# W2 loaded by column halves around batch 1's loads, half output tiles, W1's means spread between blocks, and batch 1's q transposed by DMA

## Chip, cores, metric

One core of one Trainium2 chip. The metric is the device time of one execution in microseconds (us), the median of several runs. Profiles show a span about 1 to 2 us shorter than the timed run.

## The reference

Eight batches. Attention with a memory of 32 slots per head, then a layer norm without shift and a two-layer block with residual:

```python
a = softmax(phi)                          # [8, 8, 576, 32]
k_m = einsum('bhsm,bhsd->bhmd', a, k)     # pooled keys; v_m alike
attn = softmax(q @ k_m.T / sqrt(64))
x = (attn @ v_m) -> [8, 576, 512]
xn = (x - mean) / sqrt(var + 1e-6) * g_ln
out = x + relu(xn @ w_ch1) @ w_ch2        # w_ch1 [512, 2048], w_ch2 [2048, 512]
```

## The kernel before

The kernel never forms xn: it multiplies the pooled values with W1 for each batch (w1b), corrected by the means of W1 (m_sb), and scales by the inverse deviation at the end. TensorE (PE) does for each batch: pooling (kv_ps), transposes of the pooled k and v (kvT), the w1b blocks, scores (sc_ps), denominators (den_ps), the first layer (mm1, h_ps) and, for pairs of batches, the second (mm2, ch_ps). ScalarE (ACT) and VectorE (DVE) do the copies, exponentials, additions and products between them; e are the exponentials of phi, es and hl their sums, Eh the scaled attention weights that enter the first layer. The order on each engine is the order of the program. GpSimd (POOL) issues the loads that cast fp32 to bf16, and phi of batch 1, in this order:

```python
# q, k, v of batch 0 (cut), then:
for fs in W1C:                                    # W1 in five column blocks
    nc.gpsimd.dma_start(out=w1r[:, :, fs], in_=w1_v[:, :, fs])
for n in range(4):
    w2_load(n)                                    # W2 in four row blocks of 512 KB (bf16)
phi1 = load_phi(1, nc.gpsimd)
kv1 = load_kv(1)
q1 = load_q(1)                                    # two halves
# ... and load(2): phi, k, v, q of batch 2, further down in the program
```

q has to be transposed for the scores. Batches 2 to 7 do it by DMA from SP's queue, batches 0 and 1 on PE:

```python
def a_qT(b, i):
    q_bf = loaded[b][2]
    if i == 0:
        qTs[b] = att.tile([P, 4, NP, P], BF16, name="qT")
    if b > 1:
        nc.sync.dma_start_transpose(out=qTs[b].rearrange("p j n x -> p (j n) x"),
                                    in_=q_bf.rearrange("p j n x -> p (j n x)"))
        return
    ...                                           # ten transposes on PE, then copies by ACT or DVE
```

The part of the program that the change rewrites, after batch 0's first layer:

```python
mm2(0, 0, 0, 4)          # second layer, tile 0, blocks 0 to 3 of 16; 512 columns
mm2(0, 1, 0, 4)
...
a_exp(1)                 # exponentials of phi, batch 1
mm2(0, 0, 4, 16)
mm2(0, 1, 4, 16)
mm2(0, 2, 0, 8)
a_kv(1)                  # pooling
mm2(0, 2, 8, 12)
a_tr(1)
a_qT(1, 0)
a_w1b(1, 0)
mm2(0, 2, 12, 16, finish=False)
a_qT(1, 1)
a_w1b(1, 1)
a_sc(1)                  # scores: the first use of qT
mm2_out(0, 2)
mm2(0, 3, 0, 4)
a_w1b(1, 2)
a_den(1)                 # denominators, and the products Eh
load(2)
a_exp(2)
...                      # tile 3, then mm1(1): batch 1's first layer
```

The softmax here doesn't subtract the row's maximum and nothing guards it: scores larger than these inputs give would overflow.

Of the kernel before, what the change touches and what calls it, by code (L numbers as in the profile page):

```python
# [9 lines left out]
FP32 = mybir.dt.float32  # L10
# [6 lines left out]
def kernel(  # L17
# [11 lines left out]
    nc = tc.nc  # L29
# [71 lines left out]
    w2b = consts.tile([P, JC, C], BF16, name="w2b")  # L101
    w2_v = moe_w_ch2.rearrange("(j p) c -> p j c", p=P)

    def w2_load(n):
        nc.gpsimd.dma_start(out=w2b[:, 4 * n:4 * (n + 1), :], in_=w2_v[:, 4 * n:4 * (n + 1), :])


    phi0 = load_phi(0)
# [27 lines left out]
    for fs in W1C:  # L136
        nc.gpsimd.dma_start(out=w1r[:, :, fs], in_=w1_v[:, :, fs])
    for n in range(4):
        w2_load(n)
    phi1 = load_phi(1, nc.gpsimd)  # L140
    kv1 = load_kv(1)
    q1 = load_q(1)
    loaded[1] = (phi1, kv1, q1)

    g_bf = consts.tile([P, 4], BF16, name="g_bf")
    gneg = consts.tile([P, 4, P], BF16, name="gneg")
# [37 lines left out]
    def a_exp(b):  # L184
        phi_st, kv, _ = loaded[b]
        e = att.tile([P, NS, 4, M], BF16, name="e_sb")
        nc.scalar.activation(out=e.rearrange("p c j m -> p j c m"),  # L187
                             in_=phi_st.rearrange("p j (c m) -> p j c m", m=M), func=AF.Exp)
        st8[b] = {"e": e, "kv": kv}
        if b >= 2:  # L190
            es = att.tile([P, P], FP32, name="es")
            ev = e.rearrange("p c j m -> p c (j m)")
            a4 = att.tile([P, 4, P], FP32, name="es4", bufs=1)
            nc.gpsimd.tensor_tensor(out=a4, in0=ev[:, 0:4], in1=ev[:, 4:8], op=ALU.add)  # L194
            a2 = att.tile([P, 2, P], FP32, name="es2", bufs=1)
            nc.gpsimd.tensor_tensor(out=a2, in0=a4[:, 0:2], in1=a4[:, 2:4], op=ALU.add)
            nc.gpsimd.tensor_tensor(out=es, in0=a2[:, 0], in1=a2[:, 1], op=ALU.add)
            nc.gpsimd.tensor_tensor(out=es, in0=es, in1=ev[:, 8], op=ALU.add)
            hl = att.tile([P, 2, P], BF16, name="hl")
            nc.gpsimd.tensor_copy(out=hl[:, 0], in_=es)  # L200
            nc.gpsimd.tensor_tensor(out=hl[:, 1], in0=es, in1=hl[:, 0], op=ALU.subtract)
            st8[b]["es"] = hl
# [40 lines left out]
        a_pool(b, ps)  # L243

    def a_sum(b, ps):
        if b < 2:
            kv_sum(b, ps)
        else:

            for i in range(2):  # L250
                nc.tensor.matmul(ps[:, 0, P:P + 2], st8[b]["es"][:, i, :], ones8,
                                 start=(i == 0), stop=(i == 1))
# [39 lines left out]
    def a_qT(b, i):  # L292
        q_bf = loaded[b][2]
        if i == 0:
            qTs[b] = att.tile([P, 4, NP, P], BF16, name="qT")
        if b > 1:

            nc.sync.dma_start_transpose(out=qTs[b].rearrange("p j n x -> p (j n) x"),
                                        in_=q_bf.rearrange("p j n x -> p (j n x)"))
            return  # L300
        split = b == 1 and i == 1
        if split:

            qs = [f([P, 1024], BF16, "qT_ps") for f in (big, one)]
        else:
            q_ps = big([P, 2, 1024], BF16, "qT_ps")
            qs = [q_ps[:, u, :] for u in range(2)]
        for u in range(2):
            for n in range(NP):
                nc.tensor.transpose(qs[u][:, P * n:P * (n + 1)], q_bf[:, 2 * i + u, n, :], ident)  # L310
        dst = qTs[b][:, 2 * i:2 * i + 2].rearrange("p a n x -> p a (n x)")
        if split:
            nc.scalar.activation(out=dst[:, 0], in_=qs[0][:, 0:NP * P], func=AF.Copy)
            nc.vector.tensor_copy(out=dst[:, 1], in_=qs[1][:, 0:NP * P])
        elif i == 0 or b == 1:
            nc.scalar.activation(out=dst, in_=q_ps[:, :, 0:NP * P], func=AF.Copy)
        else:
            nc.vector.tensor_copy(out=dst, in_=q_ps[:, :, 0:NP * P])
# [18 lines left out]
    def a_den(b, finish=True):  # L337
# [29 lines left out]
        if finish:  # L367
            a_den2(b)

    def a_den2(b):  # L370
        s = st8[b]
        Eh, rd = s["Eh"], s["rd"]
        for g in range(2):
            nc.scalar.activation(out=rd[:, g], in_=rd[:, g], func=AF.Exp, scale=-1.0)  # L374
            nc.vector.scalar_tensor_tensor(  # L375
                out=Eh[:, g, :], in0=s["E"][:, g, 0:S],
                scalar=s["rs"][:, g:g + 1], in1=rd[:, g].rearrange("p a x -> p (a x)"),
                op0=ALU.mult, op1=ALU.mult)

    def a_w1b(b, n, part=None):  # L380
        s = st8[b]
        if n == 0 and part in (None, 0):
            s["w1b"] = att.tile([P, 2, F], BF16, name="w1b", bufs=1)
        ps = big([P, 2, 512], FP32, "w1b_ps")
        fs = slice(512 * n, 512 * (n + 1)) if part is None else W1C[part]
        N = fs.stop - fs.start
        for j in range(4):
            for g in range(2):
                r = 64 * g
                nc.tensor.matmul(  # L390
                    ps[32 * j:32 * (j + 1), g, 0:N], s["kvT"][r:r + 64, 2, 32 * j:32 * (j + 1)],
                    w1r[r:r + 64, j, fs], start=True, stop=True, tile_position=(r, 32 * j))
        for g in range(2):
            nc.vector.scalar_tensor_tensor(  # L394
                out=s["w1b"][:, g, fs], in0=m_sb[:, fs], scalar=s["rsum"][:, g:g + 1],
                in1=ps[:, g, 0:N], op0=ALU.mult, op1=ALU.add)


    pair = {}
# [1 line left out]
    def mm1(b, j0, j1):  # L401
        s = st8[b]
        if b % 2 == 0 and j0 == 0:
            pair[b // 2] = moe.tile([P, JC, 2 * S], BF16, name="rT", bufs=1)
        rT = pair[b // 2]
        off = S * (b % 2)
        for j in range(j0, j1):
            h_ps = big([P, 2, 512], FP32, "h_ps")
            for g in range(2):
                for half in range(2):  # L410
                    nc.tensor.matmul(  # L411
                        h_ps[:, half, 0:HS], s["w1b"][:, g, P * j:P * (j + 1)],
                        s["Eh"][:, g, HS * half:HS * (half + 1)],
                        start=(g == 0), stop=(g == 1))
            dst = rT[:, j, off:off + S].rearrange("p (a x) -> p a x", a=2)
            if j % 3 != 1 if b == 0 else j % 3 or j == 0:
                nc.scalar.activation(out=dst, in_=h_ps[:, :, 0:HS], func=AF.Relu)  # L417
            else:
                nc.vector.tensor_scalar(out=dst, in0=h_ps[:, :, 0:HS], scalar1=0.0, scalar2=None,  # L419
                                        op0=ALU.max)  # L420
# [72 lines left out]
    def mm2(pr, t, j0, j1, ps=None, finish=True):  # L493
# [7 lines left out]
        if j1 == JC and finish:  # L501
            mm2_out(pr, t)

    def mm2_last(pr, t):

        x, rstd = xs[(pr, t)]
        for cs in (slice(0, 384), slice(384, 512)):
            ps = big([P, 2, 512], FP32, "last_ps")
            N = cs.stop - cs.start
            for j in range(JC):  # L510
                nc.tensor.matmul(ps[:, 0, 0:N], pair[pr][:, j, P * t:P * (t + 1)], w2b[:, j, cs],  # L511
                                 start=(j == 0), stop=(j == JC - 1))
            nc.vector.scalar_tensor_tensor(out=x[:, cs], in0=ps[:, 0, 0:N], scalar=rstd,
                                           in1=x[:, cs], op0=ALU.mult, op1=ALU.add)
            for u, queue in ((0, nc.sync), (1, nc.scalar)):
                lo = P * t + TS * u
                dst = out[2 * pr + lo // S].rearrange("(p c) x -> c p x", c=NS)
                queue.dma_start(out=dst[CO[lo % S // TS]][:, cs], in_=x[TS * u:TS * (u + 1), cs])

    def mm2_out(pr, t):  # L520
        ch_ps = chs[(pr, t)]
        x, rstd = xs[(pr, t)]
        nc.vector.scalar_tensor_tensor(out=x, in0=ch_ps, scalar=rstd, in1=x,  # L523
                                       op0=ALU.mult, op1=ALU.add)
        for u in range(2):
            lo = P * t + TS * u
            dst = out[2 * pr + lo // S].rearrange("(p c) x -> c p x", c=NS)
# [34 lines left out]
    a_w1b(0, 0, 1)  # L562
    warm(1, 256)
    mm1(0, 0, 2)
    w1_mean(2)
    m_copy(2)
    a_w1b(0, 1)
    mm1(0, 2, 5)
    w1_mean(3)
    m_copy(3)  # L570
    a_w1b(0, 2)
    mm1(0, 5, 8)
    w1_mean(4)
    m_copy(4)
    a_w1b(0, 3)
    mm1(0, 8, 11)
    a_vb(0)
    mm1(0, 11, 16)

    x_tiles(0, [0, 1])  # L580
    x_tiles(0, [2, 3])
    mm2(0, 0, 0, 4)
    mm2(0, 1, 0, 4)
    x_rstd(0, [0, 1])
    x_rstd(0, [2, 3])
    a_exp(1)
    mm2(0, 0, 4, 16)
    mm2(0, 1, 4, 16)
    mm2(0, 2, 0, 8)
    a_kv(1)  # L590
    mm2(0, 2, 8, 12)
    a_tr(1)
    a_qT(1, 0)
    a_w1b(1, 0)
    mm2(0, 2, 12, 16, finish=False)
    a_qT(1, 1)
    a_w1b(1, 1)
    a_sc(1)
    mm2_out(0, 2)
    mm2(0, 3, 0, 4)  # L600
    a_w1b(1, 2)
    a_den(1)
    load(2)
    a_exp(2)
    mm2(0, 3, 4, 12)
    a_w1b(1, 3)
    mm2(0, 3, 12, 16, finish=False)
    a_vb(1)
    mm2_out(0, 3)

    a_qT(2, 0)
    late = []
# [126 lines left out]
```

## Time and profile before

| | |
|---|---|
| time, median of 3 (range) | 250.08 us (249.71 to 250.16) |
| span of the profiled execution | 249.0 us |
| PE busy, share of the span | 95% |
| PE in the chain that ended last | 89% |
| first score matmul of batch 1 | 48.81 us |
| end of batch 1's first layer (next ch_ps) | 63.1 us |

The chain of waits is followed back from the last instruction: at each step to what released it. Time on another engine or on a DMA in that chain is time PE stood for. A transfer has landed when the trace shows it complete.

### The profile page before, as it was taken

The page shows a single profiled execution, that of the slowest core. Times are in us where ns is not written, and L with a number is a line of the kernel's source. Part 1 is how long each engine was busy: PE and PEld are TensorE (multiplying, and loading weights), DVE is VectorE, ACT ScalarE, POOL GpSimd, SP SyncE. Part 2 cuts the span into 40 slices and gives each one's busy share as a digit, 9 for nine tenths or more (in the row PEclk, how much of TensorE's full clock was granted, in tenths as well). Part 3 has the DMA queues.
Part 4 walks back from the last instruction along what each step waited for, and adds up shares of the span by engine and source line. Part 5 has one row for each costly group of instructions (what it writes and reads, how often), then busy time and mean ns, then how long its engine had stood idle before and what let it go on. Part 6 is the DMA issues. An engine that isn't in the chain of part 4 may idle for free.

```text
span 249.0 us, 5843 instructions
## 1 busy us (share of the span) xinstructions
PE 237.1 (95%) x2452; PEld 133.0 (53%) x2483; DVE 156.5 (63%) x304; ACT 129.8 (52%) x219; POOL 60.8 (24%) x100
## 2 busy tenths in 40 slices
PE   7879999999999999999999999999999999999994
PEld 2445454547644675457544674466544764476442
DVE  3228655586487655687569637685679538783641
ACT  3154583487554474838472556645580755465210
POOL 8643241014324502081206302180205001000000
PEclk9988999999999999999999999999999999999999
DMA  6999999996799799919975996629973301203133
GB/s 143 192 202 206 207 255 208 292 220 108 166 158 250 101 217 238 192 25 181 265 125 128 137 237 153 133 27 219 224 147 88 77 10 43 45 15 72 42 84 84
DMA packets 42450, 36.82 MB, mean 148 GB/s; under 512 B 17460, under 2 KB 37688, under 8 KB 42424
## 3 DMA queue, kind: packets, MB, share of 16 engines
q0 software_dynamic: 17776, 19.53, 46.9%
q1 hardware_dynamic: 24488, 16.79, 28.8%
q8 instruction: 19, 0.31, 0.5%
q10 hardware_dynamic: 160, 0.13, 0.2%
q14 instruction: 7, 0.06, 0.1%
HBM read 41.42 MB, written 9.44 MB: 204 GB/s over the span
## 4 chain that ended last, share of the span: by engine, by line
PE 89%; DMA 4%; ACT 2%; issue 2%; POOL 1%; DVE 1%; POOLq 0%
PE ch_ps L499 48%; PE h_ps L411 25%; DMA kv_bf<-in_v_dram 4%; PE w1b_ps L390 3%; PE kv_ps L210 2%; PE o_ps L442 2%; PE last_ps L511 1%; PE sc_ps L328 1%; PE m_ps L165 1%; PE den_ps L359 1%; ACT rT L417 1%; PE w_ps L179 1%; POOL q_bf L92 1%; ACT E_sb L333 1%; DVE w1b L394 1%
## 5 line engine op out<-in xcount | busy, mean ns | idle before, releaser
L499 PE MATMUL ch_ps<-w2b,rT 128*128 128x512 bf16 x531 | 123.0, 379 | 1.9 <-issue 1.1
L499 PEld LDWEIGHTS <-rT 128*128 128x128 bf16 x560 | 52.4, 98 | 63.2 <-issue 6.5
L411 PE MATMUL h_ps<-Eh,w1b 128*128 128x288 bf16 x512 | 66.3, 285 | 1.0 <-ACT rT L417 1.0
L417 ACT ACTIVATE rT<-h_ps 128x576 bf16<-128x576 f32 x88 | 52.2, 648 | 26.3 <-PE h_ps L411 26.3
L411 PEld LDWEIGHTS <-w1b 128*128 128x128 bf16 x512 | 49.5, 97 | 17.7 <-issue 2.0
L394 DVE SCALAR_TENSOR_TENSOR w1b<-m_sb,rsum,w1b_ps 128x512 bf16<-128x512 f32 (+1 forms) x66 | 44.2, 727 | 7.1 <-PE w1b_ps L390 4.7
L419 DVE TENSOR_SCALAR rT<-h_ps 128x576 bf16<-128x576 f32 x40 | 30.3, 758 | 25.3 <-PE h_ps L411 24.7
L523 DVE SCALAR_TENSOR_TENSOR x_sb<-ch_ps,rstd,x_sb 128x512 f32<-128x512 f32 x35 | 26.1, 746 | 9.7 <-PE ch_ps L499 5.4
L479 DVE BATCH_NORM_STATS2 bst<-x_sb 128x6 f32<-128x512 f32 x36 | 24.4, 678 | 8.8 <-ACT x_sb L450 8.8
L450 ACT ACTIVATE x_sb<-o_ps 128x1024 f32<-128x1024 f32 x16 | 16.0, 1027 | 18.2 <-PE o_ps L442 18.2
L287 POOL TENSOR_TENSOR vb<-v,vmask 128x256 bf16<-128x256 bf16 x12 | 7.8, 665 | 60.1 <-DVE rs L237 60.1
L194 POOL TENSOR_TENSOR es<-e_sb 128x512 f32<-128x512 bf16 x6 | 6.9, 1154 | 63.2 <-ACT e_sb L187 63.2
L485 ACT ACTIVATE rstd<-mv,eps_sb 128x2 f32<-128x2 f32 (+1 forms) x20 | 5.9, 297 | 30.5 <-DVE mv L480 30.3
L333 ACT ACTIVATE E_sb<-sc_ps,rs 128x640 bf16<-128x640 f32 x16 | 11.8, 790 | 11.8 <-PE sc_ps L328 11.8
L375 DVE SCALAR_TENSOR_TENSOR Eh<-E_sb,rs,rden 128x576 bf16<-128x576 bf16 x16 | 12.4, 815 | 8.8 <-ACT rden L374 8.8
L179 PE MATMUL w_ps<-fill 128*128 128x512 f32 (+1 forms) x16 | 10.5, 776 | 1.6 <-DVE fill L119 1.6
L390 PE MATMUL w1b_ps<-w1r,kvT 64*32 64x512 bf16 (+1 forms) x264 | 11.0, 378 | 0.2
L227 DVE CAST k<-kv_ps 128x256 bf16<-128x256 f32 x7 | 3.0, 425 | 12.5 <-PE kv_ps L210 12.5
L187 ACT ACTIVATE e_sb<-phi_st 128x1152 bf16<-128x1152 f32 x8 | 9.2, 1151 | 2.6 <-DMA phi_st<-in_phi_dram 2.6
L374 ACT ACTIVATE rden<-rden 128x576 f32<-128x576 f32 x16 | 10.0, 673 | 0.1
L92 POOL DMA_DIRECT2D q_bf<-in_q_dram x10 | 7.6, 756 | 4.6 <-DMA w2b<-in_moe_w_ch_dram 1.8
L210 PE MATMUL kv_ps<-kv_bf,e_sb 64*32 64x128 bf16 (+1 forms) x648 | 7.4, 215 | 0.6 <-DMA kv_bf<-in_v_dram 0.3
(79 smaller groups left out, 155.2 us busy)
## 6 DMA issues: line engine op xcount, KB each, us to landing
out_dram<-x_sb SPq DMA_DIRECT2D x70, 128.0 KB, 3.2
kv_bf<-in_k_dram POOLq DMA_DIRECT2D x7, 576.0 KB, 6.0
kv_bf<-in_v_dram POOLq DMA_DIRECT2D x7, 576.0 KB, 9.8
phi_st<-in_phi_dram SPq DMA_DIRECT2D x6, 576.0 KB, 5.0
q_bf<-in_q_dram POOLq DMA_DIRECT2D x6, 576.0 KB, 14.0
w2b<-in_moe_w_ch_dram POOLq DMA_DIRECT2D x4, 512.0 KB, 17.1
w1r<-in_moe_w_ch_dram POOLq DMA_DIRECT2D x3, 512.0 KB, 13.2
q_bf<-in_q_dram POOLq DMA_DIRECT2D x4, 288.0 KB, 12.8
```

The source lines that it names most:

```text
L179: nc.tensor.matmul(w_ps[:, 0:N], fill[:, 0:P], fill[:, 0:N], start=True, stop=True)
L333: nc.scalar.activation(out=E_[:, g].rearrange("p (a x) -> p a x", a=2), in_=sc[:, :, 0:HP], func=AF.Exp, scale=s["rs"][:, g:g + 1])
L375: nc.vector.scalar_tensor_tensor(out=Eh[:, g, :], in0=s["E"][:, g, 0:S], scalar=s["rs"][:, g:g + 1], in1=rd[:, g].rearrange("p a x -> p (a ...
L390: nc.tensor.matmul(ps[32 * j:32 * (j + 1), g, 0:N], s["kvT"][r:r + 64, 2, 32 * j:32 * (j + 1)], w1r[r:r + 64, j, fs], start=True, stop=Tru ...
L394: nc.vector.scalar_tensor_tensor(out=s["w1b"][:, g, fs], in0=m_sb[:, fs], scalar=s["rsum"][:, g:g + 1], in1=ps[:, g, 0:N], op0=ALU.mult, o ...
L411: nc.tensor.matmul(h_ps[:, half, 0:HS], s["w1b"][:, g, P * j:P * (j + 1)], s["Eh"][:, g, HS * half:HS * (half + 1)], start=(g == 0), stop= ...
L417: nc.scalar.activation(out=dst, in_=h_ps[:, :, 0:HS], func=AF.Relu)
L419: nc.vector.tensor_scalar(out=dst, in0=h_ps[:, :, 0:HS], scalar1=0.0, scalar2=None, op0=ALU.max)
L450: nc.scalar.activation(out=x[:, 0:n].rearrange("p i (u y) -> p i u y", u=2), in_=o_ps.rearrange("p u (i y) -> p i u y", i=2)[:, 0:n], func ...
L479: nc.vector.bn_stats(out=stt, in_=x)
L499: nc.tensor.matmul(ch_ps, rT[:, j, P * t:P * (t + 1)], w2b[:, j, :], start=(j == 0), stop=(j == JC - 1))
L523: nc.vector.scalar_tensor_tensor(out=x, in0=ch_ps, scalar=rstd, in1=x, op0=ALU.mult, op1=ALU.add)
```

## The change

The intent: with only half of W2 ahead of them, batch 1's loads land earlier, so there is time to transpose its q by DMA, which takes 20 transposes and their copies off PE, ACT and DVE. Since only W2's first 256 columns are there, the output tiles 0 to 3 are computed by halves, first halves first. W1's means are placed in smaller pieces between blocks of the first layer. Batch 1's exponential sums move to GpSimd, as in later batches.

```diff
-    def w2_load(n):
-        nc.gpsimd.dma_start(out=w2b[:, 4 * n:4 * (n + 1), :], in_=w2_v[:, 4 * n:4 * (n + 1), :])
+    C2 = (slice(0, C // 2), slice(C // 2, C))
+    def w2_load(h, n):
+        nc.gpsimd.dma_start(out=w2b[:, 4 * n:4 * (n + 1), C2[h]],
+                            in_=w2_v[:, 4 * n:4 * (n + 1), C2[h]])
@@
     for n in range(4):
-        w2_load(n)
+        w2_load(0, n)
     phi1 = load_phi(1, nc.gpsimd)
     kv1 = load_kv(1)
     q1 = load_q(1)
     loaded[1] = (phi1, kv1, q1)
+    for n in range(4):
+        w2_load(1, n)
@@ a_exp; a_sum likewise
-        if b >= 2:          # sums of the exponentials on GpSimd (es, hl)
+        if b >= 1:
@@ a_qT
-        if b > 1:           # q transposed by DMA
+        if b > 0:
@@ new: half output tiles, two halves to a bank
+    def mm2h(t, h, j0, j1):
+        if j0 == 0 and (h == 1 or t % 2 == 0):
+            halfs[h] = one([P, 2, C // 2], FP32, "ch_ps")
+        if j0 == 0:
+            chs[(t, h)] = halfs[h][:, 0 if h else t % 2, :]
+        for j in range(j0, j1):
+            nc.tensor.matmul(chs[(t, h)], pair[0][:, j, P * t:P * (t + 1)],
+                             w2b[:, j, C2[h]], start=(j == 0), stop=(j == JC - 1))
@@ W1's means, e.g.
     mm1(0, 0, 2)
-    w1_mean(2)
+    w1_mean(2, 0, 2)
+    mm1(0, 2, 3)
+    w1_mean(2, 2, 4)
     m_copy(2)
@@ the order after batch 0's first layer (new)
+    a_exp(1)
+    mm2h(0, 0, 0, 16)
+    ...                     # first halves of tiles 0 to 3
+    a_kv(1)
+    a_qT(1, 0)
+    mm2h(0, 1, 0, 4)
+    a_tr(1)
+    mm2h(1, 1, 0, 4)
+    a_w1b(1, 0)
+    load(2)
+    ...                     # second halves of tiles 0 and 1, w1b blocks 1 and 2
+    a_sc(1)
+    mm2h(2, 1, 0, 8)
+    a_den_g(1, 0)
+    mm2h(2, 1, 8, 12)
+    a_den_g(1, 1)
+    a_eh(1, 0)
+    mm2h(2, 1, 12, 16)
+    a_w1b(1, 3)
+    mm2h_out(2, 1)
+    a_eh(1, 1)
+    a_exp(2)
+    mm2h(3, 1, 0, 16)
```

Cut: the half output (mm2h_out), the split of a_den, the single banks of the last w1b block of batch 0, and a changed list of Relu blocks.

More of the change, by code (lines that the diff above doesn't have):

```diff
@@ L245, in a_sum @@
     def a_sum(b, ps):
-        if b < 2:
+        if b < 1:
             kv_sum(b, ps)
@@ L300, in a_qT @@
             return
-        split = b == 1 and i == 1
-        if split:
-            qs = [f([P, 1024], BF16, "qT_ps") for f in (big, one)]
-        else:
-            q_ps = big([P, 2, 1024], BF16, "qT_ps")
-            qs = [q_ps[:, u, :] for u in range(2)]
+        q_ps = big([P, 2, 1024], BF16, "qT_ps")
         for u in range(2):
             for n in range(NP):
-                nc.tensor.transpose(qs[u][:, P * n:P * (n + 1)], q_bf[:, 2 * i + u, n, :], ident)
+                nc.tensor.transpose(q_ps[:, u, P * n:P * (n + 1)], q_bf[:, 2 * i + u, n, :], ident)
         dst = qTs[b][:, 2 * i:2 * i + 2].rearrange("p a n x -> p a (n x)")
-        if split:
-            nc.scalar.activation(out=dst[:, 0], in_=qs[0][:, 0:NP * P], func=AF.Copy)
-            nc.vector.tensor_copy(out=dst[:, 1], in_=qs[1][:, 0:NP * P])
-        elif i == 0 or b == 1:
+        if i == 0:
             nc.scalar.activation(out=dst, in_=q_ps[:, :, 0:NP * P], func=AF.Copy)
@@ L368, in a_den, with a_den_g, a_eh, a_w1b @@
             a_den2(b)
+    def a_den_g(b, g):
+        s = st8[b]
+        if g == 0:
+            s["Eh"] = att.tile([P, 2, S], BF16, name="Eh", bufs=3)
+            s["rd"] = att.tile([P, 2, 2, HS], FP32, name="rden", bufs=1)
+        rd = s["rd"]
+        den = big([P, 2, 512], FP32, "den_ps")
+        for half in range(2):
+            o = HS * half
+            nc.tensor.matmul(den[:, half, 0:HS], blk, s["E"][:, g, o:o + HS],
+                             start=True, stop=True)
+        nc.scalar.activation(out=rd[:, g], in_=den[:, :, 0:HS], func=AF.Ln)
+        nc.scalar.activation(out=rd[:, g], in_=rd[:, g], func=AF.Exp, scale=-1.0)
+    def a_eh(b, g):
+        s = st8[b]
+        nc.vector.scalar_tensor_tensor(
+            out=s["Eh"][:, g, :], in0=s["E"][:, g, 0:S],
+            scalar=s["rs"][:, g:g + 1], in1=s["rd"][:, g].rearrange("p a x -> p (a x)"),
+            op0=ALU.mult, op1=ALU.mult)
     def a_den2(b):
         s = st8[b]
-        Eh, rd = s["Eh"], s["rd"]
+        rd = s["rd"]
         for g in range(2):
             nc.scalar.activation(out=rd[:, g], in_=rd[:, g], func=AF.Exp, scale=-1.0)
-            nc.vector.scalar_tensor_tensor(
-                out=Eh[:, g, :], in0=s["E"][:, g, 0:S],
-                scalar=s["rs"][:, g:g + 1], in1=rd[:, g].rearrange("p a x -> p (a x)"),
-                op0=ALU.mult, op1=ALU.mult)
-    def a_w1b(b, n, part=None):
+            a_eh(b, g)
+    def a_w1b(b, n, part=None, ones=False):
         s = st8[b]
@@ L383, in a_w1b @@
             s["w1b"] = att.tile([P, 2, F], BF16, name="w1b", bufs=1)
-        ps = big([P, 2, 512], FP32, "w1b_ps")
+        if ones:
+            ps = [one([P, 512], FP32, "w1b_ps") for _ in range(2)]
+        else:
+            both = big([P, 2, 512], FP32, "w1b_ps")
+            ps = [both[:, g, :] for g in range(2)]
         fs = slice(512 * n, 512 * (n + 1)) if part is None else W1C[part]
@@ L390, in a_w1b @@
                 nc.tensor.matmul(
-                    ps[32 * j:32 * (j + 1), g, 0:N], s["kvT"][r:r + 64, 2, 32 * j:32 * (j + 1)],
+                    ps[g][32 * j:32 * (j + 1), 0:N], s["kvT"][r:r + 64, 2, 32 * j:32 * (j + 1)],
                     w1r[r:r + 64, j, fs], start=True, stop=True, tile_position=(r, 32 * j))
@@ L395, in a_w1b @@
                 out=s["w1b"][:, g, fs], in0=m_sb[:, fs], scalar=s["rsum"][:, g:g + 1],
-                in1=ps[:, g, 0:N], op0=ALU.mult, op1=ALU.add)
+                in1=ps[g][:, 0:N], op0=ALU.mult, op1=ALU.add)
     pair = {}
@@ L415, in mm1 @@
             dst = rT[:, j, off:off + S].rearrange("p (a x) -> p a x", a=2)
-            if j % 3 != 1 if b == 0 else j % 3 or j == 0:
+            if j not in (1, 4, 7, 11, 14) if b == 0 else j % 3 or j == 0:
                 nc.scalar.activation(out=dst, in_=h_ps[:, :, 0:HS], func=AF.Relu)
@@ L502, in mm2, with mm2h_out @@
             mm2_out(pr, t)
+    halfs = {}
+    def mm2h(t, h, j0, j1):
[6 more added lines that the diff above has]
+                             w2b[:, j, C2[h]], start=(j == 0), stop=(j == JC - 1))
+    def mm2h_out(t, h):
+        x, rstd = xs[(0, t)]
+        nc.vector.scalar_tensor_tensor(out=x[:, C2[h]], in0=chs[(t, h)],
+                                       scalar=rstd, in1=x[:, C2[h]], op0=ALU.mult, op1=ALU.add)
+        if h == 1:
+            x_out(0, t, x)
     def mm2_last(pr, t):
@@ L524, in mm2_out, with x_out @@
                                        op0=ALU.mult, op1=ALU.add)
+        x_out(pr, t, x)
+    def x_out(pr, t, x):
         for u in range(2):
@@ L564 @@
     mm1(0, 0, 2)
-    w1_mean(2)
+    w1_mean(2, 0, 2)
+    mm1(0, 2, 3)
+    w1_mean(2, 2, 4)
     m_copy(2)
+    mm1(0, 3, 4)
     a_w1b(0, 1)
-    mm1(0, 2, 5)
     w1_mean(3)
     m_copy(3)
+    mm1(0, 4, 6)
     a_w1b(0, 2)
-    mm1(0, 5, 8)
-    w1_mean(4)
+    mm1(0, 6, 7)
+    w1_mean(4, 0, 1)
+    mm1(0, 7, 8)
+    w1_mean(4, 1, 4)
     m_copy(4)
-    a_w1b(0, 3)
-    mm1(0, 8, 11)
+    mm1(0, 8, 9)
+    a_w1b(0, 3, ones=True)
     a_vb(0)
-    mm1(0, 11, 16)
+    mm1(0, 9, 16)
     x_tiles(0, [0, 1])
     x_tiles(0, [2, 3])
-    mm2(0, 0, 0, 4)
-    mm2(0, 1, 0, 4)
+    a_exp(1)
+    mm2h(0, 0, 0, 16)
     x_rstd(0, [0, 1])
+    mm2h(1, 0, 0, 16)
+    mm2h_out(0, 0)
+    mm2h_out(1, 0)
     x_rstd(0, [2, 3])
-    a_exp(1)
-    mm2(0, 0, 4, 16)
-    mm2(0, 1, 4, 16)
-    mm2(0, 2, 0, 8)
+    mm2h(2, 0, 0, 16)
+    mm2h(3, 0, 0, 16)
+    mm2h_out(2, 0)
+    mm2h_out(3, 0)
     a_kv(1)
-    mm2(0, 2, 8, 12)
+    a_qT(1, 0)
+    mm2h(0, 1, 0, 4)
     a_tr(1)
-    a_qT(1, 0)
+    mm2h(1, 1, 0, 4)
     a_w1b(1, 0)
-    mm2(0, 2, 12, 16, finish=False)
-    a_qT(1, 1)
+    load(2)
+    mm2h(0, 1, 4, 8)
+    mm2h(1, 1, 4, 8)
     a_w1b(1, 1)
-    a_sc(1)
-    mm2_out(0, 2)
-    mm2(0, 3, 0, 4)
-    a_w1b(1, 2)
-    a_den(1)
-    load(2)
+    mm2h(0, 1, 8, 12)
+    mm2h(1, 1, 8, 12)
+    a_w1b(1, 2)
+    mm2h(0, 1, 12, 16)
+    mm2h_out(0, 1)
+    mm2h(1, 1, 12, 16)
+    mm2h_out(1, 1)
+    a_sc(1)
+    mm2h(2, 1, 0, 8)
[7 more added lines that the diff above has]
+    a_eh(1, 1)
     a_exp(2)
-    mm2(0, 3, 4, 12)
-    a_w1b(1, 3)
-    mm2(0, 3, 12, 16, finish=False)
+    mm2h(3, 1, 0, 16)
     a_vb(1)
-    mm2_out(0, 3)
+    mm2h_out(3, 1)
     a_qT(2, 0)
```

## The prediction

> **What bounds the kernel now.** I read, in this order: the shares of busy time, the 40 slices, the chain of waits from the start to 60 us, the timelines of the issuing queues, and each load's time from issue to landing. TensorE (PE) is 95% busy and holds 89% of the chain, so time is won or lost only where PE has less to do or stands waiting. The change touches nothing after 56 us except batch 2's loads and the transpose after them; the steady part keeps its order. So I need one number: when does the first block of batch 1's first layer (h_ps) start, 54.6 us now in the chain below?
>
> Chain of waits of the kernel before (start us, length us, what), in two places:
> ```profile
> 22.67 0.61 PE m_ps L165 x2
> 23.30 0.61 ACT m_sb L174
> 23.93 1.42 DVE w1b L394 x2
> 25.40 0.42 PE h_ps L411 x2
> ...
> 27.65 0.66 ACT rT L417
> ...
> 29.04 0.77 DVE rT L419
> ...
> 35.69 8.37 PE ch_ps L499 x38
> ...
> 46.13 0.57 PE qT_ps L310 x10
> ...
> 48.41 0.71 ACT qT L313
> 49.16 0.52 PE sc_ps L328 x12
> ...
> 54.62 0.57 PE h_ps L411 x4
> ```
> The reader should see that from 22 to 31 us the chain leaves PE for ACT and DVE (the means of W1 and the w1b additions), and that from 35.7 us it stays on PE with short breaks. It never goes to a load there: W2 and batch 1's loads arrive just in time. The slices show what that costs:
> ```profile
> PE   7879999999999999999999999999999999999994
> DMA  6999999996799799919975996629973301203133
> ```
> A slice is 6.2 us: the DMA engines are saturated through most of the first 56 us. The third view is the issue of two of the transposes that later batches already do by DMA, and the time to landing of each (first the one at 59.10, then the one at 85.50):
> ```profile
> 59.10 3.69 SPq L298 DMA_TRANSPOSE qT<-q_bf  x1
> ```
> ```profile
> DMA to landing us min/median/max: 5.6/5.6/5.6
> ```
> ```profile
> 85.50 9.23 SPq L298 DMA_TRANSPOSE qT<-q_bf  x1
> ```
> ```profile
> DMA to landing us min/median/max: 13.1/13.1/13.1
> ```
> The same transpose took 5.6 us when GpSimd's load queue was empty, and 13.1 us when that queue still held batch 4's k, v and q. Counting the trace's packet records by microsecond: between 91 and 94 us, 138 to 148 transpose packets of 256 B finished each us beside 137 to 141 load packets of 1152 B, one for one; at 95 us, with the loads gone, 1038 finished. A transpose has 2560 packets.
>
> **What the Trainium skill says.** "DMA: Bandwidth & Descriptors", section "Queues, rings and completion order": each DMA engine goes round between the queues that have work, at packet granularity. The trace agrees in effect: one small transpose packet per large load packet. The same page, "Issuing engines are not separate DMA queues": SP's and GpSimd's transfers share the same 16 engines. The trace agrees: loads alone finish about 180 packets of 1152 B per us (85 us, 50 to 54 us) and 140 beside the transpose. "TensorE: Matmul & The Clock Gate", section "What's actually happening": TensorE's clock falls to half after about 3.4 us of idling and needs about as long of work to rise again. The trace has a granted clock of 0.92 on average over the first 21 us, in line with one such window. The same page, "Back-to-back issue gap": about N/2.4 + 2.5 ns for N columns; the chain above has 38 matmuls of 512 columns in 8.37 us, 220 ns each, against 216.
>
> **The change part by part.**
>
> *W1's means between blocks.* From 21.4 to 34.7 us PE must do 64 h_ps matmuls at 124 ns (7.96 us per 64, a later batch's chain), 12 mean matmuls at 216 ns (2.6 us) and three w1b groups of 0.38 us: 11.7 of 13.25 us. At most 1.6 us of waiting can go; the additions of 1.42 us on DVE stay, so I take 1.0 us.
>
> *Half output tiles.* 64 matmuls of 512 columns become 128 of 256. Streaming is equal; 64 more fixed gaps of 2.5 ns are 0.16 us. Twice as many output additions on DVE (746 ns each for 512 columns) lie beside PE. Cost 0.2 us.
>
> *q of batch 1 by DMA, sums from GpSimd.* Leaves PE: 20 transposes, 2 x 0.57 us, most of the break of 0.7 us for the ACT copy at 48.41, and nine kv_sum matmuls (0.2 us). Sum 1.9 us. Added on GpSimd: es and hl, 4.1 us (from 54.85 to 58.92 in the timeline for batch 2). The exponential of batch 1 moves forward to about 37.3 us on ACT, so hl is ready near 42.6 us, when PE arrives; at most 0.3 us of waiting.
>
> If all data came in time, the sum would be -1.0 + 0.2 - 1.9 + 0.3 = -2.4 us, 247.7 us.
>
> *W2's order.* This decides. The loads land in order of issue. W1 ends at 25.6 us, as before. A 512 KB piece of W2 takes 2.55 us now (landings 28.1, 30.6, 33.2, 35.8). Half pieces have 512-byte packets, of which the first pieces of W1 finished about 380 per us; 512 of them are 1.35 us. So W2's first halves land by 31.0. Then, with the spacings of before, phi1 32.5, k1 35.2, v1 38.1, and q1 in two parts 39.5 and 40.9 us (46.6 before). SP can issue the transpose at 41.0.
>
> But behind q1 the load queue now holds W2's second halves (2048 packets, issued by 34 us since an issue waits for the landing of the eighth before it), and from 42.6 us, when GpSimd is through with es, also phi2, k2, v2 and q2 (128 large packets and 1536 of 1152 B). The transpose starts into a full queue. Before, stores issued at 40.62 into a full queue had their first packet at 44.5, the transpose alone 1.3 us after issue; here packets are smaller, so I take 2.8 us, 43.8 us. By then some 1060 of W2's packets are done. The other 984 go with one transpose packet each: (42 + 16 + 9 of switching) ns per engine, 250 per us, 3.9 us, to 47.7. Phi2's 128 take 1.7 us, to 49.4. The 1448 transpose packets left go one for one with k2, v2 and q2 at 140 per us: 10.3 us, to 59.8. If it starts at 42.3 instead, the same sum ends at 56.5. I take the landing at **58.4 us**.
>
> PE, meanwhile, gets W2's last half piece at 47.7, is done with what precedes the scores at about 49, and waits until 58.4. From there to batch 1's first layer it has 16 score matmuls (0.5 us), 32 half matmuls (3.5), four denominators (0.6) and one w1b group (0.4), 5.0 us, plus about 1.3 us because nine idle us drop the clock. Start of the first layer: 64.7 us against 54.6, **+10.1 us**, or about 260 us. W1's means and the removed transposes gain nothing then: their saving only lengthens the wait for qT.
>
> **The rivals.**
>
> *1. The transpose gets through.* If an engine serves short packets in bursts, or GpSimd reaches batch 2's loads only after the transpose, qT needs only share with W2's second halves: 41.0 us + 5.4 + 3.7 us of DMA work ends near 50 us. The scores would start at 50 instead of 48.8 and the saved work behind them makes up for it: 249 to 251 us; with a quick transpose (5.6 us, landing 46.6) 247.7. For it: the fine placing of the pieces looks like the outcome of trials. Against it: one for one over 4 us at 90 us in this very trace, and nothing that GpSimd waits for holds batch 2's loads back.
>
> *2. W2's second halves are the wait.* They may come late at 43 us, as PE reaches the second-half tiles: 1.3 us of PE work per piece against 1.35 us of DMA alone, and 2 us beside the transpose. That makes 1 to 2 us of waiting, 250 to 252 us, if the transpose isn't later still. I think it is hidden under the transpose.
>
> *3. Partial starving.* The transpose shares better with small packets and lands between 51 and 55 us: 252 to 257 us.
>
> A fourth, batch 2's loads late for batch 2, I give little: they end near 60 us, and batch 2's k and v were needed at 64.8 us even before.
>
> **Range and chances.** Starving in full I give 55 in 100 (256.5 to 263 us), part of it 15 (252 to 257), none 30 (247.5 to 251.5). The middle of that mixture is about 258 us; eight tenths lie between 248.5 and 263. Over 2% slower means over 255.1 us: 0.62. Over 2% faster, below 245.1, would need more than all removed work: 0.03. Within 2%: 0.35.
>
> **What would show it.** Right: a transpose on SP issued near 41 us with over 12 us to landing; PE waiting for that DMA by 5 us or more before sc_ps, with the clock below 1 in that slice; q1 landing near 41; W1's stage shorter by about 1 us; and everything from batch 1's first layer on as long as before. Wrong: a landing before 50 us with ch_ps running straight into sc_ps, or a wait of PE for w2b instead. The prediction fails first at the sharing rule, one packet for one, then at the time when batch 2's loads join the queue.

## The result

266.98 us (264.8 to 271.32, four runs, the longest of them slow) against 249.9 us. The ratio is 1.066 (95% interval 1.059 to 1.073). Ratios here are the mean time of one kernel's fast runs over that of the other's of the same rounds, so not quite the ratio of the medians quoted. The direction was forecast, the size was not: 17 us instead of 8, outside the range.

The slices of the page, changed kernel (a slice is 6.6 us):

```profile
PE   7879998305799999999999999999999999999994
PEclk9999999755999999999999999999999999999999
DMA  7999999995183979994697889635968210303133
```

In slices 8 to 10 (46 to 66 us) PE is busy for 3, 0 and 5 tenths and its granted clock is at 7, 5 and 5 tenths, while the DMA engines stay at 9 tenths until 60 us. The chain of waits of the changed kernel from there on:

```profile
41.19 21.02 DMA qT<-q_bf
62.21 0.14 issue
62.34 0.73 PE sc_ps L324 x16
63.08 1.82 PE ch_ps L530 x8
...
67.63 1.32 DVE w1b L412 x2
68.95 0.40 DVE x_sb L535
69.35 1.62 DVE Eh L382
70.97 0.04 issue
71.02 7.87 PE h_ps L429 x62
78.89 1.29 PE ch_ps L517 x6
```

One transfer holds the chain for 21.02 us. The costliest groups name the wait itself; the last column is PE's idle time before sc_ps and what ended it:

```profile
L324 PE MATMUL sc_ps<-qT,kvT 64*32 64x320 bf16 x128 | 4.0, 321 | 12.3 <-DMA qT<-q_bf 11.9
```

GpSimd's queue, changed kernel: W2's last half piece, then, as soon as batch 1's sums are done, batch 2's four loads, at the very time at which SP issues the transpose (41.19).

```profile
33.02 0.74 POOL L107 DMA_DIRECT2D w2b<-in_moe_w_ch_dram  x1 [0.82 <-DMA phi_st<-in_phi_dram]
...
40.47 0.43 POOL L206 TENSOR_TENSOR hl<-es,hl 128x128 bf16<-128x128 f32 x1
40.98 0.79 POOL L71 DMA_DIRECT2D phi_st<-in_phi_dram  x1
41.76 0.75 POOL L84 DMA_DIRECT2D kv_bf<-in_k_dram  x1
42.50 0.75 POOL L84 DMA_DIRECT2D kv_bf<-in_v_dram  x1
...
43.48 0.76 POOL L92 DMA_DIRECT2D q_bf<-in_q_dram  x1
```

Packets finished per us, counted in the trace's packet records of the changed kernel:

| us | W2 halves (512 B) | phi2 (4608 B) | k2, v2, q2 (1152 B) | transpose (256 B) |
|---|---|---|---|---|
| 43 | 381 | 0 | 0 | 0 |
| 45 | 98 | 56 | 4 | 76 |
| 47 | 2 | 1 | 61 | 66 |
| 49 | 0 | 12 | 95 | 109 |
| 53 | 0 | 0 | 136 | 143 |
| 57 | 0 | 0 | 140 | 144 |
| 59 | 0 | 0 | 28 | 165 |
| 61 | 0 | 0 | 2 | 156 |

Rows between are left out; at 58 us, not shown, the loads were nearly through and 446 of the transpose finished beside 71.

The three parts of the difference of 15.7 us between the two profiled spans (264.7 and 249.0): the first score matmul starts at 62.34 instead of 48.81 us, **13.5**. From there to the end of batch 1's first layer it is 16.4 us instead of 14.3, **2.1**. The rest is equal: 186.0 and 185.9 us. Two stretches by engine (busy us of each, granted clock, DMA share, which passes 1 where the records of packets overlap, GB/s), before and changed:

```profile
50.00:62.30 12.30, 12.00 (x95) 7.61 (x94) 9.37 (x15) 10.08 (x17) 3.70 (x6) 1.00 0.93 163
62.30:71.00 8.70, 8.60 (x153) 4.74 (x154) 4.61 (x14) 4.41 (x8) 3.79 (x6) 1.00 0.71 143
```
```profile
50.00:62.30 12.30, 0.47 (x3) 0.00 (x0) 0.62 (x2) 0.00 (x0) 0.00 (x0) 0.50 1.22 184
62.30:71.00 8.70, 7.19 (x62) 4.78 (x63) 4.19 (x6) 5.12 (x7) 1.72 (x2) 0.76 0.12 35
```

The clock is 0.50 while PE waits and 0.76 on average in the 8.7 us after it, where 1.00 was granted before.

### The profile page after: what moved, and what is told of

Its sections match the earlier page's. It is cut to its first block, busy times and chain, and to the rows that moved or that the text cites. A ratio compares the mean times of both kernels' runs of the same rounds, so it can differ in the third digit from the quotient of the medians.

```text
span 264.7 us, 5966 instructions
## 1 busy us (share of the span) xinstructions
PE 239.8 (91%) x2520; PEld 138.0 (52%) x2520; DVE 157.9 (60%) x307; ACT 127.8 (48%) x217; POOL 67.4 (25%) x110
## 4 chain that ended last, share of the span: by engine, by line
PE 76%; DMA 11%; DVE 4%; ACT 3%; POOL 3%; issue 1%; POOLq 0%; DVEq 0%
PE ch_ps L517 41%; PE h_ps L429 23%; DMA qT<-q_bf 8%; DMA kv_bf<-in_v_dram 4%; PE w1b_ps L408 3%; DVE w1b L412 2%; PE kv_ps L215 2%; PE o_ps L460 2%; DVE Eh L382 1%; PE last_ps L547 1%; PE sc_ps L324 1%; PE den_ps L355 1%; ACT x_sb L468 1%; PE ch_ps L530 1%; PE m_ps L170 1%
## 5 line engine op out<-in xcount | busy, mean ns | idle before, releaser
L517 PE MATMUL ch_ps<-w2b,rT 128*128 128x512 bf16 x496 | 113.5, 380 | 0.0
L517 PEld LDWEIGHTS <-rT 128*128 128x128 bf16 x496 | 46.6, 98 | 56.0 <-issue 5.7
L559 DVE SCALAR_TENSOR_TENSOR x_sb<-ch_ps,rstd,x_sb 128x512 f32<-128x512 f32 x31 | 23.1, 746 | 7.7 <-PE ch_ps L517 5.8
L382 DVE SCALAR_TENSOR_TENSOR Eh<-E_sb,rs,rden 128x576 bf16<-128x576 bf16 x16 | 13.3, 870 | 23.9 <-ACT rden L378 15.8
L199 POOL TENSOR_TENSOR es<-e_sb 128x512 f32<-128x512 bf16 x7 | 8.1, 1153 | 75.3 <-ACT e_sb L192 75.3
L468 ACT ACTIVATE x_sb<-o_ps 128x1024 f32<-128x1024 f32 x16 | 16.0, 1025 | 18.2 <-PE o_ps L460 18.2
L292 POOL TENSOR_TENSOR vb<-v,vmask 128x256 bf16<-128x256 bf16 x12 | 7.8, 665 | 60.5 <-DVE rs L242 60.5
L530 PE MATMUL ch_ps<-w2b,rT 128*128 128x256 bf16 x128 | 17.4, 292 | 2.6 <-DMA w2b<-in_moe_w_ch_dram 2.6
L530 PEld LDWEIGHTS <-rT 128*128 128x128 bf16 x128 | 12.8, 104 | 6.3 <-issue 3.4
L324 PE MATMUL sc_ps<-qT,kvT 64*32 64x320 bf16 x128 | 4.0, 321 | 12.3 <-DMA qT<-q_bf 11.9
L184 PE MATMUL w_ps<-fill 128*128 128x512 f32 (+1 forms) x16 | 9.3, 690 | 1.6 <-DVE fill L122 1.6
L192 ACT ACTIVATE e_sb<-phi_st 128x1152 bf16<-128x1152 f32 x8 | 9.2, 1152 | 2.6 <-DMA phi_st<-in_phi_dram 2.6
## 6 DMA issues: line engine op xcount, KB each, us to landing
w1r<-in_moe_w_ch_dram POOLq DMA_DIRECT2D x3, 512.0 KB, 13.9
```

The lines of the kernel that those rows point to most:

```text
L382: nc.vector.scalar_tensor_tensor(out=s["Eh"][:, g, :], in0=s["E"][:, g, 0:S], scalar=s["rs"][:, g:g + 1], in1=s["rd"][:, g].rearrange("p a ...
L468: nc.scalar.activation(out=x[:, 0:n].rearrange("p i (u y) -> p i u y", u=2), in_=o_ps.rearrange("p u (i y) -> p i u y", i=2)[:, 0:n], func ...
L517: nc.tensor.matmul(ch_ps, rT[:, j, P * t:P * (t + 1)], w2b[:, j, :], start=(j == 0), stop=(j == JC - 1))
L530: nc.tensor.matmul(chs[(t, h)], pair[0][:, j, P * t:P * (t + 1)], w2b[:, j, C2[h]], start=(j == 0), stop=(j == JC - 1))
L559: nc.vector.scalar_tensor_tensor(out=x, in0=ch_ps, scalar=rstd, in1=x, op0=ALU.mult, op1=ALU.add)
```

## The experiments

Theory A: the loss is the wait for the DMA transpose, which shares the DMA engines one packet for one with batch 2's loads, and what follows from that wait. Rivals: the halves of W2 and of the tiles cost much by themselves (B); W2's second halves are late (C); the transpose is slow by itself, or W2's small packets starve it (D). Twelve kernels ran, all with correct results. "Before" is 250.2 to 250.3 us in each of these rounds.

| run | time, us | ratio to before (95%) | qT of batch 1 landed |
|---|---|---|---|
| changed kernel | 266.98 | 1.066 (1.059 to 1.073) | 62.2 us |
| e1_q_on_pe | 253.14 | 1.012 (1.009 to 1.016) | (on PE) |
| e2_gate | 254.36 | 1.017 (1.012 to 1.022) | 49.4 us |
| e3_small_packets | 262.83 | 1.050 (1.047 to 1.054) | 57.3 us |
| e4_before_q_dma | 264.22 | 1.057 (1.053 to 1.061) | 60.5 us |
| e5_warm | 270.19 | 1.077 (1.073 to 1.082) | 62.2 us |
| e6_eh | 265.94 | 1.062 (1.058 to 1.066) | 62.6 us |
| e7_q_on_pe_eh | 251.23 | 1.004 (1.002 to 1.007) | (on PE) |
| e8_before_spread | 250.40 | 1.001 (0.999 to 1.003) | (on PE) |
| e9_warm12 | 264.40 | 1.056 (1.053 to 1.058) | 61.8 us |
| e10_warm12_eh | 264.09 | 1.055 (1.053 to 1.058) | 62.7 us |
| e11_gate_q2_first_eh | 253.31 | 1.012 (1.010 to 1.014) | 50.1 us |
| e12_before_spread_hl | 250.11 | 1.000 (0.998 to 1.002) | (on PE) |

With a threshold of 2%, e1, e7, e8, e11 and e12 count as the same as before, e2 as unclear, the others as slower; the smaller differences below are read from these intervals and from the traces.

### e1_q_on_pe: the DMA transpose undone

```diff
-        if b > 0:
+        if b > 1:
@@
-    a_qT(1, 0)          # after a_kv(1)
+    a_qT(1, 0)          # before a_w1b(1, 0), on PE
+    a_qT(1, 1)          # before a_w1b(1, 1)
```

> The changed kernel with only one part undone: q of batch 1 is transposed on TensorE again (two blocks of ten transposes, before the first and the second w1b group), so no DMA transpose is in flight beside batch 2's loads. Theory A (the loss is the wait for the DMA transpose and what follows from it): the 11.9 us wait of sc_ps goes, 247 to 250 us. Rival B (the halves of W2 and the half output tiles cost much by themselves, and would be seen as waits on W2 and more instructions): stays above 256 us. Rival C (W2's second halves are late): a wait of PE for w2b of 1 to 2 us stays, 250 to 252 us.

253.14 us: some 14 us of the 17 go with this one part, but the result lies 3 us above what theory A gave. The chain of waits shows where, in this run:

```profile
55.22 1.60 DVE Eh L382
56.83 0.04 issue
56.87 7.87 PE h_ps L429 x62
```

DVE's second Eh product comes after the last w1b additions and an output addition and is slow; batch 1's first layer waits 2.1 us for it. PE further stands 0.9 us before the first second-half tile, and 0.6 us for DVE's addition of an output (x_sb) later. The 0.9 us are put down to DVE at the matmul, but its weight load waited 1.0 us for w2b. In this run DVE's work and that piece of W2 ended together (42.70 us); e2 parts them: DVE was done at 42.45, the piece landed at 42.74, and PE went on at 42.79. So it is rival C, at 0.9 us, and the rest is rival B: the rearrangement costs by itself, by waits for DVE as well as for W2.

### e7_q_on_pe_eh: the same, with Eh earlier on DVE

```diff
     mm2h(2, 1, 12, 16)
+    a_eh(1, 1)
     a_w1b(1, 3)
     mm2h_out(2, 1)
-    a_eh(1, 1)
```

> q of batch 1 on TensorE (as in the earlier run of that part, 253.1 us) and the second Eh product ahead of the last w1b additions. If the 3 us that this run stayed above the kernel before are mostly the stop for Eh, it is now 250.5 to 251.5 us; if the half tiles and W2's halves cost more than that, it stays over 252 us.

251.23 us, as expected. The second Eh now takes 0.82 us (in the timeline of DVE, this run) where it took 1.67 in e1 and 1.70 in the changed kernel:

```profile
53.96 0.82 DVE L382 SCALAR_TENSOR_TENSOR Eh<-E_sb,rs,rden 128x576 bf16<-128x576 bf16 x1 [0.44 <-ACT rden L378]
```

The slow ones ran while GpSimd added batch 2's exponentials (from 69.20 us in the changed kernel, Eh from 69.26). In e2, where GpSimd came to them later (56.39 us), Eh in the same late place took 0.81. GpSimd was slowed too: its second addition took 1.12 us beside Eh, 0.73 in a later batch of the same run. This fits what the Trainium skill says in "SBUF — State Buffer", section "SBUF: two separate sides": a DVE instruction with two SBUF inputs and a GpSimd instruction that reads SBUF exclude each other for their whole length. Even so mended, the arrangement is 0.4% over the kernel before, with 0.8 us for W2's first second-half piece and 0.6 us for DVE left.

### e2_gate: batch 2's loads held back

```diff
+    tok = consts.tile([P, 1], BF16, name="tok")
+    nc.gpsimd.tensor_copy(out=tok, in_=qTs[1][:, 3, NP - 1, 0:1])
     load(2)
```

> The changed kernel with batch 2's loads held back: GpSimd first copies one element of batch 1's qT, so it issues phi2, k2, v2 and q2 only after the DMA transpose has landed. Theory A (starved by batch 2's loads, one packet for one): the transpose starts near 45 us, when W2's second halves are nearly through, and then runs alone at about 900 packets per us, landing at 48.5 to 50 us instead of 62.2; PE waits under 2 us; 249 to 252 us. Rival D (the transpose is slow by itself, or W2's small packets starve it): it lands after 55 us, over 257 us. Batch 2's loads end near 60 us in either case; if they are then late for batch 2, a new wait of PE for kv_bf or e_sb near 64 us shows.

Time from issue to landing of the transpose in this run, in place of 21.0 us:

```profile
DMA to landing us min/median/max: 7.9/7.9/7.9
```

It landed at 49.4 us, as theory A said, though W2's second halves were still queued when it was issued: at 44 us, 286 of their packets finished beside the first 206 of the transpose, at 47 us 985 transpose packets. Rival D falls. The total missed the expected 249 to 252: the wait moved on. Batch 2's q, delayed by the gate, was transposed late, and the scores of batch 2 waited for it:

```profile
66.66 6.79 DMA qT<-q_bf
73.45 0.04 issue
73.49 0.47 PE sc_ps L324 x16
```

Before the change too the DMA engines were full up to 56 us (the slices in the prediction): what one transfer gained in order here, another lost.

### e3_small_packets: how the engines share

```diff
-        nc.gpsimd.dma_start(out=t[:, js, slot, :], in_=rows(src, b)[:, js, :])
+        for xs_ in ([slice(192 * i, 192 * (i + 1)) for i in range(3)] if b == 2 else [slice(0, NS * D)]):
+            nc.gpsimd.dma_start(out=t[:, js, slot, xs_], in_=rows(src, b)[:, js, xs_])
         # and the same for q
```

> The changed kernel with batch 2's k, v and q loaded in thirds of a row: the same bytes in three times as many packets of 384 B instead of 1152 B, nothing held back. If engines share packet for packet, [...]the transpose lands at 56 to 58 us instead of 62.2 although the loads themselves get no faster: 261 to 263 us. If they share by bytes or by time, the transpose lands at 62 us or later, 266 us or more.

The transpose landed at 57.3 us, 4.9 us sooner, although the loads beside it got slower, not faster (they ended after 61 us):

```profile
DMA to landing us min/median/max: 16.4/16.4/16.4
```

From 50 to 55 us, 275 to 288 transpose packets finished per us beside 272 to 279 load packets of 384 B; in the changed kernel it was 135 to 155 beside 129 to 143 of 1152 B. One for one in both. So while the two share the engines, the rate of the transpose follows its neighbour's packets, not its own bytes. The total, 262.83 us, lies in the expected range. It fell by less than the landing, since from the scores to the end of the layer it took 18.2 us here: the stop for Eh came, 2.1 us, and the clock stayed low (0.86 from 63.5 us on).

### e4_before_q_dma: this part alone, in the kernel before

```diff
-        if b > 1:
+        if b > 0:
@@
-    a_qT(1, 1)
```

> The kernel before with one part of the change alone: q of batch 1 transposed by DMA in place of the 20 transposes on TensorE; W2 whole, full tiles, means as they were. Theory A: q1 lands at 46.6 us, batch 2's loads are queued behind it, the transpose starts near 50 us and lands at 59 to 62 us against 48.8 when the scores start now: 260 to 265 us. Rival D (it needs W2's small second halves to starve it): it lands by 54 us, under 256 us.

264.22 us. With W2 whole, tiles whole and means as they were, the DMA transpose alone costs 14 us. The chain of waits, this run:

```profile
28.20 19.29 DMA q_bf<-in_q_dram
...
47.58 12.91 DMA qT<-q_bf
```

From 52 to 54 us it was 143 to 145 transpose packets beside 139 to 140 loads. This run and e1 tell the same from both sides. Bringing q forward by W2's halves gained nothing: the transpose was issued at 41.19 instead of 47.58 us and landed at 62.2 instead of 60.5.

### e5_warm and e9_warm12: the clock after the wait

```diff
     mm2h_out(1, 1)
+    warm(19)            # e9: warm(12)
     a_sc(1)
```

> The changed kernel with 19 idle-time matmuls (128x512 fp32 of zeros, some 10.6 us) put before batch 1's scores, so that TensorE stays busy while it waits for the transpose; nothing else changed. If the halved clock after the wait is part of the loss: the transpose lands as before (61 to 63 us), but the time from the first score matmul to the end of batch 1's first layer falls from 16.4 us by 1.2 to 1.5 us, with a granted clock of 1.0 there instead of 0.76. If the clock costs nothing there (ACT and DVE set the pace), it stays within 0.3 us.

> The changed kernel with 12 idle-time matmuls before batch 1's scores. In the run with 19 they took 0.9 us each, 17.7 us in all, and ended after the transpose had landed; 12 should end near 61 us, before it. The transpose lands at 61 to 63 us as before. If the halved clock is part of the loss, the time from the first score matmul to the first matmul of batch 1's first layer falls from 6.8 to 4.8 us (as in the gated run, at full clock), and from 16.4 us to 14.5 or so up to the end of that layer, unless the stop for Eh drops the clock again.

e5 missed by my sizing: I took 0.56 us for a matmul of 128x512 fp32, but the 19 stand in the trace as 38 records, two to a matmul, 17.77 us in all, and ended at 68 us, after the transpose. With 12 they ended near 61.5 us. In e9 the stretch after the wait ran at full clock:

```profile
62.30:71.00 8.70, 6.61 (x69) 5.17 (x62) 5.45 (x8) 6.30 (x10) 3.31 (x5) 1.00 0.16 37
```

The first matmul of batch 1's first layer came 4.8 us after the scores instead of 6.8, and the end of the layer 15.05 us after them instead of 16.38. So the dropped clock cost 1.9 us at the first mark and 1.3 us at the second; the rest went into a longer stop for Eh (2.1 us instead of 1.5). The total fell with it, to 264.40 us.

### e6_eh and e10_warm12_eh: Eh's place

The edit is the one of e7, on the changed kernel; e10 adds warm(12).

> The changed kernel with one line of DVE's order changed: batch 1's second Eh product is put ahead of the last w1b additions and an output addition. In the changed kernel it came after them, took 1.70 us beside GpSimd's es additions instead of 0.8, and batch 1's first layer stood 1.5 us after its first two matmuls. Expected: Eh takes 0.8 us again, that stop goes, and the time from the first score matmul to the end of batch 1's first layer falls from 16.4 us by 1.7 to 2.0 us. If the order is not the cause, the stop only moves to another wait.

> Both: 12 idle-time matmuls before the scores, and the second Eh product ahead of the last w1b additions. If clock and Eh together are all that the changed kernel loses after the landing, the time from the first score matmul to the end of batch 1's first layer is 12.8 to 13.5 us (16.4 in the changed kernel, 14.2 in the one before), and the total 2.5 to 3.5 us under the changed kernel, 262.5 to 264.5 us.

In e6 Eh took 0.82 us and the stop after two matmuls went, but the layer ended only 0.7 us sooner after the scores (15.6 instead of 16.4): a miss; the first matmul of the layer came 7.5 us after them instead of 6.8. In e10, at full clock, it ended 13.9 us after them, 1.1 less than in e9 and slightly more than the expected 12.8 to 13.5. The first layer then stops later, in the timeline of this run:

```profile
69.48 2.13 PE L429 MATMUL h_ps<-Eh,w1b 128*128 128x288 bf16 x16 [0.42 <-DVE w1b L412]
71.81 5.15 PE L429 MATMUL h_ps<-Eh,w1b 128*128 128x288 bf16 x40 [0.20 <-DVE rT L437]
```

DVE has w1b, an output and vb (the masked pooled values) to do in the same two us, so moving Eh ahead moves part of the stop to the others. Together clock and Eh explain 2.5 us, all that the changed kernel had lost after the landing (2.1) and a little more. The totals of e9 and e10 do not differ, since in e10 the transpose landed 0.9 us later.

### e8_before_spread and e12_before_spread_hl: the small parts alone

e8 puts the changed kernel's order of W1's means, with the two single banks and the Relu list, into the kernel before; e12 adds the sums on GpSimd and moves batch 1's exponentials ahead of the second layer's first tiles.

> The kernel before with W1's means spread between blocks alone (with the two single banks for the last w1b block and the changed list of Relu blocks). Prediction's term: 1.0 us less, 248.7 to 249.4 us, ratio 0.995 to 0.998. If the shorter stage in the changed kernel came only from the clock window that fell elsewhere (0.92 in the first 21 us of one profile, 1.00 in the other), the ratio is 1.000 within 0.002.

> The kernel before with W1's means spread (which alone gave a ratio of 1.001) and batch 1's exponential sums from GpSimd. Prediction's term: nine matmuls, 0.2 us less. Expected ratio 0.998 to 1.001; PE then waits for batch 1's v or q instead, which land at 42.9 and 46.6 us.

Neither gains anything that shows: 1.001 and 1.000. The first h_ps matmul and the first o_ps matmul after batch 0's first layer, in the timeline of the kernel before and of e8:

```profile
21.26 1.14 PE L411 MATMUL h_ps<-Eh,w1b 128*128 128x288 bf16 x8
...
34.60 0.72 PE L442 MATMUL o_ps<-vb,Eh 64*128 64x128 bf16 x16
```
```profile
19.29 0.41 PE L415 MATMUL h_ps<-Eh,w1b 128*128 128x288 bf16 x2
...
32.64 0.83 PE L446 MATMUL o_ps<-vb,Eh 64*128 64x128 bf16 x16
```

13.34 us before, 13.35 in e8 (13.51 in the changed kernel). The whole stage is earlier in e8's profile because a window of half clock lay at 17 to 20 us in the profile of before (0.66 granted from 16 to 21 us) and not in this one. Of those 2 us only 0.5 are left at batch 1's first layer (53.94 against 54.46): PE then waits for batch 1's v and q, 0.5 us each, whose landing had been hidden.

### e11_gate_q2_first_eh: a try at a version that beats both

```diff
+        if b == 2:
+            p2 = load_phi(b, nc.gpsimd)
+            q2 = load_q(b)               # q ahead of k and v
+            loaded[b] = (p2, load_kv(b), q2)
+            return
```

with the gate of e2 and the Eh of e7.

> An attempt at a version that beats both: batch 2's loads held back until batch 1's q has been transposed, batch 2's q loaded ahead of its k and v so that its transpose starts early, and Eh's order mended. The gated run lost 3.4 us waiting for batch 2's transpose at 70 us and 1.6 us for Eh. Expected 248.7 to 250.0 us. If k2 and v2, now last and beside the transpose, land after 64 us, a wait of PE for kv_bf takes the place, 250 to 253 us.

253.31 us, a miss. Batch 2's scores no longer wait long, but batch 1's transpose landed at 50.1 us:

```profile
40.90 9.24 DMA qT<-q_bf
```

PE waited 2.4 us for it, twice what it waited in e2. The scores started at 50.28, at a lowered clock (a score matmul took 456 ns instead of 296), and DVE's queue stopped the first layer as in e10. No version here beats the kernel before.

## Why the prediction failed

**The mechanism was right.** Starved by batch 2's loads, one packet for one: e1 and e4 show the transpose to be the loss, e2 shows that batch 2's loads make it long, e3 shows the sharing. Rival 1 (it gets through) and rival 3 fall. Of rival 2, a wait of 2.0 us for W2's last half piece is in the trace, hidden under the transpose as said, and one of 0.5 us for its first; with q left on PE (e1, e7) the latter is 0.8 to 0.9 us and no longer hidden.

**The size was wrong.** The sum was +10.1 us at the start of batch 1's first layer. Measured there it is +14.7 (69.13 us against 54.46): of the gap of 4.6, 3.8 are the landing and 0.5 the way from the scores to the layer. Within the layer 0.9 more was lost. The failed terms:

- *The start of the transpose, "2.8 us, 43.8 us": measured 4.2 us after the issue, 45.4.* In e2, where only W2's halves were queued, it was 2.6. The trace that the prediction read had such a delay: the transpose issued at 85.50 us had its first packet 4.5 us later. And W2's halves began at 39 us, not 41, so 1536 and not 1060 of their packets were done at 43.8. By itself this does not explain the miss: at 45.4 us only 59 packets of W2, 98 of phi2 and the 1536 of k2, v2 and q2 were left for 2560 of the transpose, so the loads run out first. With the prediction's own rates, and 1038 per us for the 867 packets without a partner, the landing would be 58.7 us, an estimate.
- *The rates, and so the landing, 58.4 us: measured 62.2, 3.8 us short.* This is the step that failed. The middle, 135 to 155 per us, was as taken, but the sum has no slow stretches. From 46 to 50 us 66 to 123 packets of the transpose finished per us, fewer than the 140 taken. From 59.0 us on, with 52 load packets left, the last 495 took until 61.7 us, 156 to 174 per us, and the landing came 0.5 us after the last packet. By these counts the first stretch cost some 0.8 us and the second some 2.2, both estimates.
- *From the scores to the layer, 6.3 us with 1.3 for the clock: measured 6.8.* The work was right (4.8 at full clock in e9, 5.0 taken); the clock cost 1.9. Missing was what followed: the new order on DVE, with Eh behind the w1b additions, then doubled beside GpSimd, which stopped the layer for 1.5 us. It stands in the diff, and I read the order of PE alone.
- *The pull of rival 1.* I gave 30 in 100 to a quick transpose on the ground that the fine placing of pieces looks like the outcome of trials. That moved the stated time from about 260 to 258 and no run supports it.
- *Slips in the sums.* 42 + 16 + 9 ns per engine (16 engines over 380 and 1038 packets per us, and what the pairs at 140 leave) is 239 pairs per us, not 250. And the chances as given put over nine tenths between 248.5 and 263 us, not eight. Neither decides anything.

**Terms that did not matter to the result and were wrong or right.** W1's means, 1.0 us less: measured nothing (e8). Half tiles, 0.2 us in matmuls: 64 took 7.09 us in e1's chain, 111 ns each, against 110 for half of a full one; right, but with W2's order they brought 0.6 us of waiting for DVE and 0.8 to 0.9 us for W2's piece (e1, e7); the first I had not counted. q landing at 40.9 us: the transpose was issued at 41.19, right. Nothing after batch 1's first layer changed: 186.0 and 185.9 us, right.

**What stays open:** why the last 500 packets of the transpose ran at some 160 per us at 59 to 61 us, when alone 1000 finish. The packets themselves were slow, 70 to 115 ns each on average against 31 before. Stretches like it stand in the other runs (46 us in e2, 316 packets of 102 ns; 46 to 48 us in e3, 84 to 90 ns), but in e2 and e3 not at the end. No run shows what slows them, and the records do not name the engine. Open too is why the first packet came 4.2 us after the issue here and 2.6 in e2.

## What to carry to other kernels

In these runs a transfer of many small packets beside a queue of larger ones was not served by its share of the bytes: it finished about one packet for each of its neighbour's, 140 per us beside 1152 B and 280 beside 384 B, as long as the queue lasted. Before moving work from an engine to a DMA transpose, look at what the load queue holds from issue to need; here it was not empty, and the engine was the cheaper place (e1, e4). And where loads fill the stretch, a new order can move the wait from one tile to the next (e2).

## What the Trainium skill lacked or had wrong

- "DMA: Bandwidth & Descriptors", "Queues, rings and completion order", says that an engine drains a whole packet of some 9 to 17 descriptors before it switches queue. The counts per us are equal in the trace's own packet records, 140 of 256 B beside 140 of 1152 B and 280 beside 275 of 384 B; they can't tell bursts of equal length from strict alternation, but what it means for time, landing after 21.0 us instead of 5.6, is not on the page.
- The same page, "Rules for kernel authors", says a transpose next to ordinary DMAs needs nothing. Results were correct in every run; what the page leaves out is time, which wants an empty queue: 5.6 us alone, 7.9 beside the rest of W2, 12.9, 16.4 and 21.0 beside loads.
- The same page, "Latency and other measured facts", gives some 600 ns to the first byte of such a transfer. Here 1.3 us passed from the start of the issue to the first packet with an empty load queue, and 2.6 to 4.2 us with a full one (e2, e4, e3, changed kernel). The page does not say what it counts from.
- "SBUF — State Buffer", "SBUF: two separate sides", was borne out in effect; it gives no figure for such a pair, and this is one: 1.67 to 1.70 us for Eh beside GpSimd's additions against 0.82.
